# Four moves in a fused attention and MLP kernel: x emptied ahead of the masks, two stores held back, larger pieces of w_in, scores ahead of outputs

## The chip, the cores and the metric

The kernel runs on one core of a Trainium2 chip. The metric is the device time of one execution in microseconds, and less is better. Three runs of the kernel before gave a median of 215.4 us (215.04 to 215.58). One more execution, taken with the hardware profiler, took 215.47 us; every row of the trace quoted below is from that one.

## The reference

Decayed linear attention is computed over blocks, its heads are put side by side to give x of 3072 tokens by 512, and x goes through a two-layer MLP with an exact GELU. With B = 4, H = 8, S = 768, D = 64:

```python
for b in range(nb):                       # blocks of 64 positions
    intra = (qb @ kb^T * Dmask) @ vb      # lam**(i-j) below the diagonal
    inter = (qb * lam**(pos+1)) @ kv_state
    out[:, :, sl] = intra + inter
    kv_state = lam**64 * kv_state + (kb * lam**(63-pos))^T @ vb
x = out.transpose(0, 2, 1, 3).reshape(B * S, H * D)
h = x @ w_in                              # 512 x 2048
g = 0.5 * h * (1 + erf(h / sqrt(2)))
return g @ w_out                          # 2048 x 512
```

## The kernel before, in words

The sequence is cut into six groups of 128 positions. A group g holds four chunks n = 4g to 4g+3, one for each batch element. Attention of a chunk ends in a quarter (128 columns) of the transposed tile x of its group. The MLP of a group is a list of blocks, each one stretch of TensorE work: 16 blocks `mm1` (four matmuls each, then a GELU on ScalarE into `g_t`), perhaps a `rest` block for columns left out of the first `mm1` blocks, and 16 blocks `mm2` (four matmuls each; every fourth finishes 128 rows of output, which ScalarE copies to `o_sb` and SyncE's queue stores).

The order on every engine is written by hand (`manual_schedule`): each engine runs its instructions in program order. `run_blocks` walks the blocks of group g and calls, ahead of block i, whatever a dictionary lists for i. So attention of group g+1 lies between the MLP blocks of group g.

A *visit* `visit(f, d)` issues two chunks' attention matmuls in alternation: of chunk d the scores `sc` and the state products `kv`, of chunk f the outputs `o` (from its state, its masked scores `sm`, and its state in mid-chunk `mid`). VectorE then works on what the visit left in PSUM, in program order: `mask(d)` (L232), the sum `t` (L247) and its copy `mid` (L251), `empty(f)` (L284: `o` times `lam_o` into x), and the next state (L256, L258). The last visit of a group stands ahead of its last `mm2` block, and fills the last quarter of the next x.

Before a state product, GpSimd must have made `vd`, the decayed v of the chunk (L221, `decay_v`), and half of `k2`, a copy of k by half blocks (L208). From group 1 on, v of a whole group comes in four loads (`load_blocks`, L81), called V1 to V5 below; `decay_v` of any chunk of the group waits for all four.

All loads are issued by GpSimd (POOL), which also turns float32 into bf16 on the way; the list in `ask` gives their order at the start: the k, q and v of group 0, pieces of w_in (each in two halves of the partitions, L100), four pieces of w_out (L103), then k4, q4, V1, k5, q5 and so on. SyncE's queue (SP) carries the stores (L381) and, from chunk 8 on, the DMA transposes of k and q (L198, L199), in one order: two stores of group 0, the transposes of chunk 8, the other two stores of group 0, the transposes of chunk 9, and on. Each SP entry waits for its source, and all behind it wait as well.

The start (group 0) has its own forms: `scores0`, `outputs0`, `transposed` on TensorE, and matmuls on zeros (`keep_warm`, L422) that fill gaps. The first two `mm1` blocks of group 0 leave out the last 128 columns (n3 = 2), which a `rest` block adds later; `mm1` block 2 is the first that needs all four chunks of x.

Of the kernel before, what the change touches and what calls it, by code (L numbers as in the profile page):

```python
# [8 lines left out]
F32 = mybir.dt.float32  # L9
# [6 lines left out]
def kernel(  # L16
# [10 lines left out]
    nc = tc.nc  # L27
# [3 lines left out]
    C = 128  # L31
    L = 64
    NB = S // C
    HP = H // 2
# [19 lines left out]
    def bank(shape, dtype, tag, name):  # L54
        return ps.tile(shape, dtype, tag=tag, name=name, bufs=BANKS[tag])

    def half(i):
        return slice(i * 64, (i + 1) * 64)
# [9 lines left out]
    def load(n, name):  # L68
        g, b = n // B, n % B
        t = raw[n, name] = qkv_pool.tile([128, H, D], BF16, tag=name, name=f"{name}_t",  # L70
                                         bufs=B if name == "v" else 10)
        nc.gpsimd.dma_start(t, dram[name][b, :, g * C:(g + 1) * C, :].rearrange("h si d -> si h d"))  # L72

    def load_blocks(g):

        t = raw["group", g] = qkv_pool.tile([128, 2, B * HP, D], BF16, tag="vg", name="vg_t", bufs=3)
        src = v.rearrange("b (hp hi) s d -> hi s (b hp) d", hi=2)
        for u in range(2):
            for hi in range(2):
                s = g * C + u * L  # L80
                nc.gpsimd.dma_start(t[half(hi), u], src[hi, s:s + L])  # L81
# [23 lines left out]
    def ask(items):  # L105

        for item in items.split():
            name, at = item[0], item[1:]
            if name in "kqv":
                load(int(at), name)  # L110
            elif name == "V":
                load_blocks(int(at))
            else:
                (load_w_in if name == "i" else load_w_out)(*(int(x) for x in at.split("-")))

    ask("k0 q0 k1 q1 v0 k2 q2 v1 k3 q3 v2 i0-2 v3 i2-3 i3-5 i5-8 i8-12 i12-16 o0-4 o4-8 o8-12 o12-16 "
        "k4 q4 V1 k5 q5 k6 q6 k7 q7")

    idle = consts.tile([128, 512], BF16)
# [54 lines left out]
    live = {}  # L174
# [59 lines left out]
    def states(c):  # L234
        kv = c.kv = bank([128, 2, HP, D], F32, "at", "kv_ps")
        us = range(2) if c.g < NG - 1 else range(1)
        return [[(kv[half(hi), u, hp, :], c.k2[half(hi), u, hp, :], vd[c.n][half(hi), u, hp, :], True)
                 for hi in range(2)] for u in us for hp in range(HP)]
# [44 lines left out]
    def empty(c):  # L283
        nc.vector.tensor_mul(xT[c.g][:, :, c.b * C:(c.b + 1) * C], c.o, lam_o)  # L284

    def issue(*lists):

        for i in range(max(map(len, lists))):
            for pairs in lists:
                if i < len(pairs):  # L290
                    for out_, lhsT, rhs, start in pairs[i]:
                        nc.tensor.matmul(out_, lhsT, rhs, start=start, stop=True, skip_group_check=True)  # L292

    def visit(f, d, hold=False):
        f, d = (live[n] if n is not None else None for n in (f, d))
        lists = []
        if d:
            kv = states(d)
            lists.append(scores(d) + kv)
        if f:  # L300
            lists.append(outputs(f))
        issue(*lists)
        if d is None:
            empty(f)
            f = None
        if d:
            mask(d)
            next_states(d, lambda: f and empty(f), hold)


    def scores0(n):
        c = live[n]
        sc = [bank([128, HP, C], F32, "at", f"sc{hi}_ps") for hi in range(2)]
        issue([[(sc[hi][:, hp, :], c.kT[half(hi), hp, :], c.qT[half(hi), hp, :], True) for hi in range(2)]
               for hp in range(HP)])
        c.sm = work_pool.tile([128, HP, 2, C], BF16, tag="sm0", name="sm0")
        dmask_r = dmask0.rearrange("p (hp hi) i -> p hp hi i", hi=2)
        for hi in range(2):
            nc.vector.tensor_mul(c.sm[:, :, hi, :], sc[hi], dmask_r[:, :, hi, :])

    def outputs0(n):
        c = live[n]
        c.o = bank([128, HP, C], F32, "at", "o_ps")
        issue([[(c.o[half(1 - hi), hp, :], c.v[:, 2 * hp + hi, :], c.sm[:, hp, hi, :], True) for hi in range(2)]
               for hp in range(HP)])
# [4 lines left out]
        eng.tensor_mul(c.kd, c.k, lam_m[:, :, None].to_broadcast((128, H, D)))  # L330

    xT = {}

    def alloc_x(g):
        xT[g] = x_pool.tile([128, NK1, T], BF16, tag="x", name="x_t")
# [12 lines left out]
    def mlp(g, n3):  # L348

        x_t = xT[g]  # L350
        g_t = g_pool.tile([128, NK2, T], BF16, tag="g", name="g_t")

        def mm1(kf, hi=T):
            def run():
                h_ps = bank([128, T], F32, "mh", "h_ps")
                cuts = [(0, 2 * C), (2 * C, hi)] if g < 2 and kf == 0 else [(0, hi)]
                for lo, up in cuts:
                    for ki in range(NK1):
                        nc.tensor.matmul(h_ps[:, lo:up], w_in_t[:, ki, kf * 128:(kf + 1) * 128], x_t[:, ki, lo:up],  # L359
                                         start=(ki == 0 and lo == 0), stop=(ki == NK1 - 1), skip_group_check=True)  # L360
                nc.scalar.activation(g_t[:, kf, :hi], h_ps[:, :hi], ACT.Gelu)  # L361
            return run

        def rest(kfs):
            def run():
                h_ps = bank([128, len(kfs), C], F32, "mh", "h_ps")
                for i, kf in enumerate(kfs):
                    for ki in range(NK1):
                        nc.tensor.matmul(h_ps[:, i, :], w_in_t[:, ki, kf * 128:(kf + 1) * 128], x_t[:, ki, T - C:],
                                         start=(i == 0 and ki == 0), stop=(ki == NK1 - 1), skip_group_check=True)  # L370
                nc.scalar.activation(g_t[:, kfs[0]:kfs[-1] + 1, T - C:], h_ps, ACT.Gelu)
            return run

        om = {}

        def store(io, ps_, w):
            n = w.stop - w.start
            o_sb = out_pool.tile([128, n], F32, tag=f"o_{n}", name="o_sb")
            r = io * S + g * C
            nc.scalar.copy(o_sb, ps_)  # L380
            nc.sync.dma_start(out[r:r + C, w], o_sb)  # L381

        def mm2(io, part):
            def run():
                if part == 0:
                    om[io] = bank([128, d_model], F32, "mo", "o2_ps")
                for kf in range(part * 4, part * 4 + 4):
                    nc.tensor.matmul(om[io], g_t[:, kf, io * C:(io + 1) * C], w_out_t[:, kf, :],  # L388
                                     start=(kf == 0), stop=(kf == NK2 - 1))
                if part == NK2 // 4 - 1:  # L390
                    store(io, om[io], slice(0, d_model))
            return run

        def mm2_half(io, h):
            def run():
                w = slice(h * (d_model // 2), (h + 1) * (d_model // 2))
                o2 = bank([128, d_model // 2], F32, "mo", "o2_ps")
                for kf in range(NK2):
                    nc.tensor.matmul(o2, g_t[:, kf, io * C:(io + 1) * C], w_out_t[:, kf, w],  # L399
                                     start=(kf == 0), stop=(kf == NK2 - 1))  # L400
                store(io, o2, w)
            return run

        blocks = [mm1(kf, T - C if kf < n3 else T) for kf in range(NK2)]
        late = [rest(list(range(i, min(i + 4, n3)))) for i in range(0, n3, 4)]
        blocks = blocks[:n3 + 2] + late + blocks[n3 + 2:]
        if g == 0:
            blocks += [mm2(io, part) for pair in range(0, B, 2) for part in range(4) for io in (pair, pair + 1)]
        elif g == NG - 1:
            blocks += [mm2(io, part) for io in range(B - 1) for part in range(4)]  # L410
            blocks += [mm2_half(B - 1, h) for h in range(2)]
        else:
            blocks += [mm2(io, part) for io in range(B) for part in range(4)]
        return blocks
# [3 lines left out]
    def keep_warm(n, new=True):  # L418
        if new:
            idle_ps[0] = bank([128, 512], F32, "mo", "idle_ps")  # L420
        for _ in range(n):
            nc.tensor.matmul(idle_ps[0], idle[:, :128], idle, start=True, stop=True)  # L422
# [25 lines left out]
    transposed(live[3], "q", "mo", nc.scalar)  # L448
    make_lam()
    nc.scalar.activation(warm, pos, ACT.Gelu)  # L450
    outputs0(2)
    empty(live[2])
    keep_warm(1)
    scores0(3)
    keep_warm(2, new=False)


    n3 = 2
# [36 lines left out]
    visit(6, None)  # L495
    live[6].rest()
    visit(None, 7)

# [95 lines left out]
```

## Time and profile before

| what | value |
|---|---|
| median of 3 runs | 215.4 us (215.04 to 215.58) |
| profiled execution | 215.47 us |
| its span, first to last instruction | 213.7 us |
| TensorE busy (PE) | 200.6 us, 94% |
| VectorE (DVE), ScalarE (ACT), GpSimd (POOL) busy | 80.2, 90.0, 108.9 us |
| loads, queue of GpSimd | 13.64 MB, 80256 packets |
| stores and transposes, queue of SyncE | 10.50 MB, 21152 packets |
| mean granted TensorE clock | 0.989 of full speed |

Times in a view are microseconds from the first instruction. In the timeline a row has start, duration, engine, line, operation, operands and count, and in brackets how long the engine was idle before it and what ended that. In the chain of waits a row has start, length and what the time went to. A DMA issue is listed with the time from issue to landing. A table by windows has, for each stretch, its length, each engine's busy time and count of instructions, the granted TensorE clock, the DMA share, and GB/s.

### The profile page before, as it was taken

What the parts mean: (1) busy time and instruction counts of PE and PEld (TensorE: products, weight loads), DVE (VectorE), ACT (ScalarE), POOL (GpSimd) and SP (SyncE); (2) the same over time, 40 slices, a digit from 0 to 9 for tenths busy, and PEclk for the clock granted to TensorE, in tenths of its full rate; (3) what the DMA queues carried; (4) which work ended last, traced back from release to release, by engine and by line L of the source; (5) the groups of instructions that cost most, each with busy time, mean ns of one, the idle gap of its engine ahead of it and who ended that gap; (6) DMA issues with size and microseconds to landing.
All of it is one profiled execution on the core that took longest, in us unless ns stands there. A gap on an engine that the chain in (4) does not pass through costs nothing.

```text
span 213.7 us, 5227 instructions
## 1 busy us (share of the span) xinstructions
PE 200.6 (94%) x2241; PEld 99.7 (47%) x2241; DVE 80.2 (38%) x176; ACT 90.0 (42%) x161; POOL 108.9 (51%) x152
## 2 busy tenths in 40 slices
PE   7679999969999999999999799999999999999993
PEld 2345444436654444444444344444444544444452
DVE  5759102219715565725633816532330330100000
ACT  6555671429565411356311356311366221576121
POOL 8999643789759973999679969400000000000000
PEclk9969999999999999999999999999999999999998
DMA  6999999999999999999999999712100012100112
GB/s 39 145 157 162 198 206 198 155 211 94 187 109 143 139 162 127 82 148 222 165 150 133 221 180 160 80 52 98 52 2 3 0 52 98 49 3 0 49 52 95
DMA packets 101431, 24.46 MB, mean 114 GB/s; under 512 B 93600, under 2 KB 98464, under 8 KB 101408
## 3 DMA queue, kind: packets, MB, share of 16 engines
q0 software_dynamic: 80256, 13.64, 87.8%
q1 hardware_dynamic: 21152, 10.50, 24.1%
q8 instruction: 17, 0.28, 0.5%
q14 instruction: 6, 0.05, 0.1%
HBM read 27.27 MB, written 6.29 MB: 157 GB/s over the span
## 4 chain that ended last, share of the span: by engine, by line
PE 72%; DMA 11%; POOL 10%; DVE 3%; issue 1%; ACT 1%; POOLq 0%
PE h_ps L359 32%; PE o_ps L388 32%; DMA w_out_t<-in_moe_w_out_dram 7%; DMA q_t<-in_q_dram 4%; POOL w_in_t L100 3%; PE sc_ps L292 3%; PE o_ps L292 2%; POOL k_t L72 2%; POOL q_t L72 2%; POOL v_t L72 2%; PE o_ps L399 2%; PE kv_ps L292 1%; POOL w_out_t L103 1%; DVE x_t L284 1%; DVE sm L232 1%
## 5 line engine op out<-in xcount | busy, mean ns | idle before, releaser
L359 PE MATMUL h_ps<-x_t,w_in_t 128*128 128x512 bf16 (+3 forms) x392 | 84.9, 372 | 2.1 <-DVE x_t L284 1.6
L388 PE MATMUL o_ps<-w_out_t,g_t 128*128 128x512 bf16 x368 | 82.8, 379 | 0.0
L361 ACT ACTIVATE g_t<-h_ps 128x512 bf16<-128x512 f32 (+1 forms) x96 | 56.6, 591 | 35.5 <-PE h_ps L359 35.5
L359 PEld LDWEIGHTS <-w_in_t 128*128 128x128 bf16 x392 | 37.1, 98 | 44.3 <-issue 3.7
L388 PEld LDWEIGHTS <-g_t 128*128 128x128 bf16 x368 | 34.9, 98 | 40.8 <-issue 0.2
L380 ACT COPY o_sb<-o_ps 128x512 f32<-128x512 f32 (+1 forms) x25 | 14.1, 570 | 70.5 <-PE o_ps L388 68.0
L232 DVE TENSOR_TENSOR sm<-sc_ps,dmask 128x512 bf16<-128x512 f32 x20 | 13.8, 690 | 70.8 <-PE sc_ps L292 70.8
L221 POOL TENSOR_TENSOR vd<-vg_t,lam_v 128x512 bf16<-128x512 bf16 x20 | 20.9, 1047 | 15.0 <-DMA vg_t<-in_v_dram 11.8
L72 POOL DMA_DIRECT2D k_t<-in_k_dram x24 | 21.9, 910 | 2.9 <-DMA w_out_t<-in_moe_w_out_dram 2.1
L72 POOL DMA_DIRECT2D q_t<-in_q_dram x24 | 21.6, 899 | 2.3 <-DMA w_out_t<-in_moe_w_out_dram 1.9
L284 DVE TENSOR_TENSOR x_t<-o_ps,lam_o 128x512 bf16<-128x512 f32 x24 | 16.4, 682 | 9.1 <-PE o_ps L292 9.1
L81 POOL DMA_DIRECT2D vg_t<-in_v_dram x20 | 16.6, 846 | 4.3 <-DMA w_out_t<-in_moe_w_out_dram 2.8
L208 POOL COPY k<-k_t 64x256 bf16<-64x256 bf16 x38 | 15.7, 412 | 1.1
L212 DVE COPY k<-k_t 64x256 bf16<-64x256 bf16 x34 | 12.1, 356 | 0.5
L292 PEld LDWEIGHTS <-kT 64*64 64x64 bf16 (+1 forms) x352 | 7.7, 108 | 8.3 <-issue 7.9
L292 PE MATMUL sc_ps<-qT,kT 64*64 64x64 bf16 (+1 forms) x352 | 10.6, 199 | 0.5 <-ACT qT L193 0.5
L292 PE MATMUL o_ps<-sm,vg_t 64*64 64x64 bf16 x320 | 8.8, 193 | 0.1
L292 PE MATMUL kv_ps<-vd,k 64*64 64x64 bf16 x288 | 8.4, 193 | 0.3 <-ACT k L212 0.3
L258 DVE TENSOR_TENSOR state<-t,lam_c 128x256 bf16<-128x256 f32 x16 | 8.2, 511 | 0.5
L422 PE MATMUL idle_ps<-idle 128*128 128x512 bf16 x17 | 6.8, 517 | 1.2 <-DVE idle L120 1.2
L100 POOL DMA_DIRECT2D w_in_t<-in_moe_w_in_dram x12 | 7.6, 676 | 0.4 <-DMA v_t<-in_v_dram 0.2
L292 PEld LDWEIGHTS <-vg_t 64*64 64x64 bf16 x320 | 7.0, 108 | 0.2 <-issue 0.2
(62 smaller groups left out, 119.3 us busy)
## 6 DMA issues: line engine op xcount, KB each, us to landing
out_dram<-o_sb SPq DMA_DIRECT2D x23, 256.0 KB, 4.2
k_t<-in_k_dram POOLq DMA_DIRECT2D x24, 128.0 KB, 6.0
q_t<-in_q_dram POOLq DMA_DIRECT2D x24, 128.0 KB, 5.8
vg_t<-in_v_dram POOLq DMA_DIRECT2D x20, 128.0 KB, 8.0
w_out_t<-in_moe_w_out_dram POOLq DMA_DIRECT2D x4, 512.0 KB, 12.9
w_in_t<-in_moe_w_in_dram POOLq DMA_DIRECT2D x4, 256.0 KB, 7.3
v_t<-in_v_dram POOLq DMA_DIRECT2D x4, 128.0 KB, 4.8
w_in_t<-in_moe_w_in_dram POOLq DMA_DIRECT2D x4, 128.0 KB, 4.9
```

What stands on the lines that cost most here:

```text
L72: nc.gpsimd.dma_start(t, dram[name][b, :, g * C:(g + 1) * C, :].rearrange("h si d -> si h d"))
L81: nc.gpsimd.dma_start(t[half(hi), u], src[hi, s:s + L])
L100: nc.gpsimd.dma_start(w_in_t[half(1 - hi), :, f], w_in_r[hi, :, :, f])
L208: same.tensor_copy(c.k2[half(hi), hi], k_r[half(hi), :, hi, :])
L221: nc.gpsimd.tensor_mul(vd[n], of_group(n), lam_vb)
L232: nc.vector.tensor_mul(c.sm, c.sc, dmask)
L284: nc.vector.tensor_mul(xT[c.g][:, :, c.b * C:(c.b + 1) * C], c.o, lam_o)
L292: nc.tensor.matmul(out_, lhsT, rhs, start=start, stop=True, skip_group_check=True)
L359: nc.tensor.matmul(h_ps[:, lo:up], w_in_t[:, ki, kf * 128:(kf + 1) * 128], x_t[:, ki, lo:up], start=(ki == 0 and lo == 0), stop=(ki == NK1 ...
L361: nc.scalar.activation(g_t[:, kf, :hi], h_ps[:, :hi], ACT.Gelu)
L380: nc.scalar.copy(o_sb, ps_)
L388: nc.tensor.matmul(om[io], g_t[:, kf, io * C:(io + 1) * C], w_out_t[:, kf, :], start=(kf == 0), stop=(kf == NK2 - 1))
```

## The change

It has four parts.

1. **w_in.** The pieces i2-3 and i3-5 (columns 256 to 384 and 384 to 640) become one piece i2-5. Two DMA issues on GpSimd go, and two stay that are larger.
2. **x emptied first.** In a visit with both chunks, `empty(f)` comes ahead of `mask(d)`, the sum and `mid` on VectorE if f is of group 2 or later. For f of group 1 the order stays.
3. **Stores held back.** The four stores of group 0 are put on SP's queue after the last visit of group 0's MLP: behind the transposes of chunk 8, which wait for k8 and q8. Before, two of them stood ahead of these.
4. **Scores of chunk 3.** `scores0(3)` goes ahead of `outputs0(2)` on TensorE, its mask stays behind `empty(2)` on VectorE, and three matmuls on zeros that stood around it go.

```diff
-    ask("k0 q0 k1 q1 v0 k2 q2 v1 k3 q3 v2 i0-2 v3 i2-3 i3-5 i5-8 i8-12 i12-16 o0-4 o4-8 o8-12 o12-16 "
+    ask("k0 q0 k1 q1 v0 k2 q2 v1 k3 q3 v2 i0-2 v3 i2-5 i5-8 i8-12 i12-16 o0-4 o4-8 o8-12 o12-16 "
         "k4 q4 V1 k5 q5 k6 q6 k7 q7")
...
         issue(*lists)
-        if d is None:
+        if d is None or f and f.g > 1:
             empty(f)
             f = None
...
-    def scores0(n):
+    def scores0(n, mask=True):
         c = live[n]
-        sc = [bank([128, HP, C], F32, "at", f"sc{hi}_ps") for hi in range(2)]
+        c.sc = [bank([128, HP, C], F32, "at", f"sc{hi}_ps") for hi in range(2)]
...
+        if mask:
+            mask0(n)
+
+    def mask0(n):
+        c = live[n]
         c.sm = work_pool.tile([128, HP, 2, C], BF16, tag="sm0", name="sm0")
...
+    held = []
+
+    def store_held():
+        for r, w, o_sb in held:
+            nc.sync.dma_start(out[r:r + C, w], o_sb)
...
             nc.scalar.copy(o_sb, ps_)
-            nc.sync.dma_start(out[r:r + C, w], o_sb)
+            if g == 0:
+                held.append((r, w, o_sb))
+            else:
+                nc.sync.dma_start(out[r:r + C, w], o_sb)
...
     nc.scalar.activation(warm, pos, ACT.Gelu)
+    scores0(3, mask=False)
     outputs0(2)
     empty(live[2])
-    keep_warm(1)
-    scores0(3)
-    keep_warm(2, new=False)
+    mask0(3)
...
     visit(6, None)
     live[6].rest()
     visit(None, 7)
+    store_held()
```

More of the change, by code (lines that the diff above doesn't have):

```diff
@@ L308, in visit @@
             next_states(d, lambda: f and empty(f), hold)
-    def scores0(n):
+    def scores0(n, mask=True):
         c = live[n]
-        sc = [bank([128, HP, C], F32, "at", f"sc{hi}_ps") for hi in range(2)]
-        issue([[(sc[hi][:, hp, :], c.kT[half(hi), hp, :], c.qT[half(hi), hp, :], True) for hi in range(2)]
+        c.sc = [bank([128, HP, C], F32, "at", f"sc{hi}_ps") for hi in range(2)]
+        issue([[(c.sc[hi][:, hp, :], c.kT[half(hi), hp, :], c.qT[half(hi), hp, :], True) for hi in range(2)]
                for hp in range(HP)])
+        if mask:
+            mask0(n)
+    def mask0(n):
+        c = live[n]
         c.sm = work_pool.tile([128, HP, 2, C], BF16, tag="sm0", name="sm0")
@@ L318, in scores0 @@
         for hi in range(2):
-            nc.vector.tensor_mul(c.sm[:, :, hi, :], sc[hi], dmask_r[:, :, hi, :])
+            nc.vector.tensor_mul(c.sm[:, :, hi, :], c.sc[hi], dmask_r[:, :, hi, :])
     def outputs0(n):
```

## The prediction

> **What bounds the kernel now.** The page comes first: TensorE is busy for 94% of the span, so what can be won is in its gaps, 13.1 us of 213.7.
>
> ```profile
> PE 200.6 (94%) x2241; PEld 99.7 (47%) x2241; DVE 80.2 (38%) x176; ACT 90.0 (42%) x161; POOL 108.9 (51%) x152
> ```
>
> Where the gaps lie is read from TensorE's timeline: the bracket of a row is its idle time and what ended it. Three rows concern this change.
>
> ```profile
> 46.34 0.40 PE L191 MATMUL t_ps<-ident,q_t 128*128 128x128 bf16 x4 [1.84 <-DMA q_t<-in_q_dram]
> ...
> 120.52 1.67 PE L359 MATMUL h_ps<-x_t,w_in_t 128*128 128x512 bf16 x7 [1.15 <-DVE x_t L284]
> ...
> 151.85 1.45 PE L359 MATMUL h_ps<-x_t,w_in_t 128*128 128x512 bf16 x6 [0.49 <-DVE x_t L284]
> ```
>
> The last two stand where group 2 gives way to 3, and 3 to 4: the first `mm1` block needs the last quarter of x. The chain of waits, in order of time, says what VectorE does in the first of them.
>
> ```profile
> 118.16 0.69 DVE sm L232
> 118.85 0.34 DVE t L247
> ...
> 119.21 0.66 DVE mid L251
> 119.87 0.61 DVE x_t L284
> ```
>
> Mask, sum and copy of a chunk that nobody needs for 8 us run ahead of the x that TensorE waits for.
>
> The third view is GpSimd's timeline in group 1, with the chain's rows for the state products that need its work.
>
> ```profile
> 60.84 1.04 POOL L221 TENSOR_TENSOR vd<-vg_t,lam_v 128x512 bf16<-128x512 bf16 x1 [3.65 <-DMA vg_t<-in_v_dram]
> 61.83 0.85 POOL L208 COPY k<-k_t 64x256 bf16<-64x256 bf16 x2
> ...
> 67.35 0.85 POOL L208 COPY k<-k_t 64x256 bf16<-64x256 bf16 x2
> ```
>
> ```profile
> 63.38 0.25 PE kv_ps L292 x16
> ...
> 68.43 0.03 PE kv_ps L292 x2
> ```
>
> GpSimd waits 3.65 us for V2 and from there works without a gap until 68.20 (67.35 + 0.85). TensorE's kv of chunk 8 starts 0.70 after GpSimd's copy for it (62.68), and kv of chunk 9 only 0.23 after its copy (68.20). So the landing of V2 is hidden now, but by 0.2 us.
>
> **Part 2, x first.** Nothing is added or removed; two rows of order change. At 118, the outputs end at about 118.4 (last row of the visit 118.18 + 0.22). `empty` then takes 0.68 and x is ready at 119.15. TensorE's `mm2` block began at 118.33 and its four matmuls are issued at 0.216 each, so the next can start at 119.20 instead of 120.52: 1.32 won (the row says 1.15 of idle, since it counts from the modelled end of the matmul before). At 150, `mm2` began at 150.32 and is through at 151.19 against 151.85: 0.66. Sum 1.98, by the brackets alone 1.64; I take 1.9. At the turn from 1 to 2 two `mm2` blocks follow the visit and no wait is seen; from 4 to 5 there is no chunk d. What is pushed back, by `empty`'s 0.68 and about 0.25 of waiting for the outputs, is sm, t, mid and state of d; they are next read in a visit 6 or more blocks on (at 0.86 each, 5 us), and the PSUM banks that they free are asked for there too. Price: nothing, while those 5 us stand.
>
> **Part 3, the stores.** Two stores are issued at 39.94 and 40.80. k5, issued at 35.70, lands after 8.4 (44.1); q5, at 38.51, after 7.8 (46.3); k6, at 39.38, after 7.8 (47.2). Loads otherwise land 0.85 apart, so the two stores cost the loads 2.2 - 0.85 = 1.4 us, 0.7 each. Held back, q5 and all loads behind it land 1.4 earlier, and the 1.84 bracket at 46.34 shrinks by so much.
>
> But the gain has to pass GpSimd. Its chain from 43.39 (first vd of group 1, on V1's landing) to the issue of V2 at 52.10 has no gap and does not wait for these loads; it does not move. V2's four loads are issued from 52.10 to 55.38, as before, and the last lands at about 60.7. Into them now fall the held stores. On SP's queue they wait for the transposes of chunk 8: k8 lands near 49.6, q8 (issued at 47.12, and 3.9 us is the shortest landing of such a load) at 51.0; at 1.25 of issue each the queue is free at 52.3, and four stores follow at about 0.55 to 0.6. Stores 2 and 3 were there before (54.75, 55.23); 0 and 1 are new. The window from 51 to 54 is nearly empty and takes some of them:
>
> ```profile
> 43.00:47.00 4.00, 2.11 (x33) 1.08 (x33) 0.00 (x0) 0.82 (x2) 3.54 (x5) 1.00 1.94 231
> 51.00:54.00 3.00, 3.00 (x81) 1.62 (x80) 2.39 (x6) 2.86 (x7) 2.94 (x6) 1.00 0.47 94
> 57.00:61.00 4.00, 3.59 (x40) 2.00 (x34) 2.01 (x6) 2.73 (x6) 0.35 (x2) 1.00 1.90 222
> ```
>
> (The last three columns are clock, DMA share, GB/s.) A store alone lands 2.0 after its issue (those after 171 us), so store 0 is through by 54.4, before V2's bytes; store 1 mostly collides. V2's delay lies between -0.7 (store 2 slips behind it) and +1.4 (both new ones in front); I take +0.1 to +0.5 with part 1 counted, nearer the first end because of the idle window. The Trainium skill (DMA: Bandwidth & Descriptors, "Issuing engines are not separate DMA queues") says that DMAs of all queues interleave on the same 16 engines, which speaks against this part: held stores meet other loads; by that rule alone the delay is 1.4. Nobody else waits behind these stores: the next SP entry, the transpose of k9, waits for k9 at 61.5 anyway, and four of six `o_sb` buffers are held until long before the next store at 78.8.
>
> **Part 1, w_in.** GpSimd saves two issues of 0.61, 1.2 us; no load lands earlier for it, since they already queue (i5-8 lands 5.5 and 5.8 after issue, the first loads 3.9): price 0, at best -1.2. For the DMA engines: i2-3 and i3-5 landed from 17.7 to 19.8, 2.1 for 384 KB; the one pair of the new form, i5-8, took 19.8 to 22.3, 2.5. So all later loads, V1 too, slip by 0.4 (0 to 0.4), and GpSimd's chain with them; that is in V2's +0.5. `mm1` block 2 now needs the whole piece, at 17.7 + 2.5 = 20.2, where it started at 19.29 behind x: TensorE 0.9 late. The wait for q5 hides it; without that, 0.9.
>
> **Part 4, scores.** TensorE does `scores0(3)` at 15.2 (qT is copied by 15.16) in the wait for v2, and loses three matmuls of zeros. VectorE masks chunk 3 behind `empty(2)` as before, from 16.72, and the first piece of w_in still lands at 16.8 (11.72 and 5.1): nothing moves, price 0. The danger is the clock.
>
> ```profile
> 7.72:11.13 3.41, 2.06 (x35) 1.28 (x32) 2.79 (x5) 1.72 (x3) 3.41 (x5) 1.00 2.29 146
> 11.13:14.55 3.42, 3.35 (x30) 1.90 (x28) 1.82 (x4) 1.05 (x2) 3.42 (x7) 0.50 2.09 155
> 14.55:17.96 3.41, 2.34 (x28) 1.49 (x29) 2.34 (x4) 2.61 (x8) 3.09 (x6) 1.00 1.68 163
> ```
>
> After 3.41 us with 2.06 of work the clock stood at 0.50 for as long. The third stretch loses about 0.6 of its 2.34 and falls below 2.06, so the next may run at half: between 0 and 1.7 us of TensorE (3.41 / 2), about 0.6 on top of the 0.9, as it waits for w_in in much of that stretch. [...]
>
> **Sum.** TensorE comes to q5 0.9 to 1.5 late, q5 lands 1.0 earlier (1.4 - 0.4); of the bracket of 1.84 nothing or little is left, and TensorE is 0.4 to 1.0 ahead. At kv of chunks 8 and 9 GpSimd decides: V2's delay of 0.1 to 0.5 less the 0.2 of slack, 0 to +0.3. After chunk 12 GpSimd runs a chunk or more ahead, so the shift stays. Front +0.2, turns -1.9: 1.7 off the profiled execution of 215.47 (span 213.7, 1.8 around it), which is 0.07 over the median: 213.8, span 212.0.
>
> **Rivals.**
> - *The front gains too.* V2 lands up to 0.7 earlier because the stores fit in 51 to 54 or slip behind it. kv of chunk 9 can then come 0.2 to 0.9 earlier: 212.8 to 213.5. For it: DMA share 0.47 there. Against: it needs part 1 to cost nothing.
> - *The stores meet V2.* Delay 1.4 + 0.4, less 0.2: +1.6, less 1.9: 215.1. For it: the 1.4 that two stores cost at 44. Within the noise of the kernel before.
> - *Slower: the clock falls in the wait for V2.* TensorE, ahead by up to 1.0, stops at kv of chunk 8 for that and V2's delay, 1.5 to 2.8 in one place near 62; if 3.41 us hold no more than 2.06 of work, the next run at half, in dense matmuls that nothing hides: 1.7. With V2's delay of 1.4 to 1.8: 216.5 to 216.8. It decides from a stop of 1.35 on. Against: the stop of 1.84 at 44.5, in a stretch with 2.11 of 4.00, left the clock at 1.00.
> - That parts 3 or 4 do not happen is excluded by the order of the queues; that part 2 wins nothing needs another wait at 119.2, and none is seen (h_ps's banks are free).
>
> **Numbers.** Main case 58% (213.2 to 214.5), front gains 15%, stores meet V2 17%, clock 10%. A measurement of this kernel tells about 0.3%, 0.65 us: below 214.75 is faster. The first two lie there, 73%; the third is within, 17%; the last is slower, 10%. The range takes in the first three: 212.9 to 215.1.
>
> **What would show it.** Right: no bracket at the turns to groups 3 and 4; the bracket at q5 below 0.8; GpSimd's first vd of group 1's own plan (60.84) at 60.9 to 61.4, still after a wait for V2; a bracket of 0.5 to 1.5 at kv of chunk 8. Wrong: V2 landing after 62, a clock of 0.5 after 21.4, or a new bracket of over 0.3 in groups 2 to 5.

## The result and the profile after

The changed kernel took 214.52 us (median of 20 runs, 213.0 to 216.07) where the kernel before, run beside it, took 215.52 (20 runs). The ratio is 0.9944 with a 95% interval of 0.9917 to 0.997, which lies below 1: about 1.2 us less (0.0056 x 215.5), small but faster. Here and below a median is over all executions of a kernel, while a ratio and its interval leave out those that took over 1.5% longer than its fastest. The profiled execution took 213.86 us (span 212.1), against 215.47 (span 213.7) before.

The page of the kernel after begins so; its PE row lacks a few records (2211 matmuls, where 2238 weight loads are listed), so its 92% is too low:

```profile
span 212.1 us, 5187 instructions
PE 195.4 (92%) x2211; PEld 98.7 (47%) x2238; DVE 80.6 (38%) x176; ACT 89.9 (42%) x161; POOL 107.6 (51%) x150
```

**The turn from group 2 to 3.** The chain in order of time, kernel after. Where before VectorE's sm, t, mid and x stood between the visit and `mm1`, there is now only TensorE's own queue:

```profile
118.80 0.16 issue
118.96 0.81 PE o_ps L401 x3
119.77 2.40 PE h_ps L369 x11
```

VectorE's timeline, kernel after: x is first, and mask and sum come behind it.

```profile
118.90 0.69 DVE L284 TENSOR_TENSOR x_t<-o_ps,lam_o 128x512 bf16<-128x512 f32 x1 [3.71 <-PE o_ps L292]
119.50 0.68 DVE L232 TENSOR_TENSOR sm<-sc_ps,dmask 128x512 bf16<-128x512 f32 x1
120.10 0.42 DVE L247 TENSOR_TENSOR t<-kv_ps,state 128x256 f32<-128x256 f32 x1
```

From the visit before the turn to the one behind it, TensorE needs 7.68 us (118.09 to 125.77) where it needed 8.99 (117.66 to 126.65): 1.31 won. At the turn from 3 to 4 it is 7.65 (148.73 to 156.38) against 8.30: 0.65 won.

**The front.** TensorE's timeline, kernel after, with the brackets that carry it:

```profile
19.87 1.89 PE L369 MATMUL h_ps<-x_t,w_in_t 128*128 128x512 bf16 x7 [1.13 <-DMA w_in_t<-in_moe_w_in_dram]
...
44.55 0.39 PE L191 MATMUL t_ps<-ident,q_t 128*128 128x128 bf16 x4
...
62.91 0.77 PE L292 MATMUL kv_ps<-vd,k 64*64 64x64 bf16 x16 [1.33 <-POOL k L208]
...
68.85 0.22 PE L292 MATMUL sc_ps<-qT,kT 64*64 64x64 bf16 x2 [0.75 <-DMA qT<-q_t]
```

The first row is part 1's wait for the larger piece of w_in. The second is q5's transpose: the 1.84 that stood there before is gone. The third is the wait at kv of chunk 8, which the prediction had. The fourth, at the scores of chunk 9, it did not have. The chain in order of time shows where that one comes from:

```profile
55.21 9.06 DMA q_t<-in_q_dram
64.28 0.02 issue
64.29 4.52 DMA qT<-q_t
68.81 0.04 issue
68.85 0.22 PE sc_ps L292 x2
```

q9's load took 9.06 us to land (6.1 before). Then come its DMA transpose on SP's queue, 4.52 (3.56 before), and TensorE. GpSimd's timeline has the issue of V2 and its first use, in the vd of chunk 8: first the kernel before, whose vd stood at 60.84, then the kernel after.

```profile
52.10 3.31 POOL L81 DMA_DIRECT2D vg_t<-in_v_dram  x4
```

```profile
51.04 3.30 POOL L81 DMA_DIRECT2D vg_t<-in_v_dram  x4
...
61.48 1.04 POOL L221 TENSOR_TENSOR vd<-vg_t,lam_v 128x512 bf16<-128x512 bf16 x1 [5.36 <-DMA vg_t<-in_v_dram]
```

So V2 is issued 1.06 earlier and used 0.64 later: from issue to use it takes 10.44 us, where it took 8.74.

The visit of chunk 10 is 0.8 later than before in these two profiles (74.77 against 73.94), and the visit ahead of the first turn 0.4 (118.09 against 117.66). From chunk 10's visit to the end the kernel after needs 137.3 us where the kernel before needed 139.8. So in the profiles the back gains about 2.4 and the front loses 0.8: 1.6, the difference of the spans (213.7 - 212.1). One profile of each is little for the front: in three profiles with part 2 alone or a piece of it (below), whose start is that of the kernel before, this visit begins at 73.75, 74.81 and 74.82.

### The profile page after: what moved, and what is told of

Same layout as the page of the kernel before. It is cut to its first block, busy times and chain, and to the rows that moved or that the text cites. A ratio compares the mean times of both kernels' runs of the same rounds, so it can differ in the third digit from the quotient of the medians.

```text
span 212.1 us, 5187 instructions
## 1 busy us (share of the span) xinstructions
PE 195.4 (92%) x2211; PEld 98.7 (47%) x2238; DVE 80.6 (38%) x176; ACT 89.9 (42%) x161; POOL 107.6 (51%) x150
## 4 chain that ended last, share of the span: by engine, by line
PE 74%; POOL 12%; DMA 9%; issue 1%; ACT 1%; POOLq 0%
PE o_ps L401 34%; PE h_ps L369 34%; DMA q_t<-in_q_dram 4%; DMA w_in_t<-in_moe_w_in_dram 3%; POOL k_t L72 3%; PE sc_ps L292 2%; DMA qT<-q_t 2%; POOL q_t L72 2%; POOL vd L221 2%; POOL v_t L72 2%; PE o_ps L412 2%; POOL vg_t L81 2%; PE o_ps L292 1%; PE kv_ps L292 1%; POOL k L208 1%
## 5 line engine op out<-in xcount | busy, mean ns | idle before, releaser
L401 PE MATMUL o_ps<-w_out_t,g_t 128*128 128x512 bf16 x354 | 80.0, 379 | 1.7 <-issue 1.6
L212 DVE COPY k<-k_t 64x256 bf16<-64x256 bf16 x34 | 13.0, 381 | 0.5
L292 PEld LDWEIGHTS <-k 64*64 64x64 bf16 x288 | 6.5, 108 | 2.2 <-POOL k L208 1.7
L247 DVE TENSOR_TENSOR t<-kv_ps,state 128x256 f32<-128x256 f32 x16 | 6.7, 416 | 1.6 <-PE kv_ps L292 1.5
```

Of the source, the lines that this page charges most:

```text
L212: copy(c.k2[half(hi), 1 - hi], k_r[half(1 - hi), :, hi, :])
```

## The experiments

The theory after the result: part 2 earns its two us at the turns; part 1 brings the loads forward; and part 3 loses what that earns, since the held stores run beside V2, k9 and q9 and make the transposes of chunk 9 late. Then the whole without part 3 should be the best of all. The rival: group 1's loads and transposes are late as a set, whatever is moved among them, so that what is won at one wait only comes back at the next. The first four kernels take the change apart. All ran beside the kernel before (median 215.29).

### Part 2 alone

```
-        if d is None:
+        if d is None or f and f.g > 1:
             empty(f)
```

> Part 2 alone: x is emptied ahead of the masks from group 2 on, all else as before. Theory A (the turns pay): the brackets of 1.15 and 0.49 us at the turns to groups 3 and 4 go, nothing else moves; 1.6 to 2.0 us less than before, ratio 0.991 to 0.9925. Theory B (the gain of the whole change comes from the start, group 0 and 1): the turns are worth at most 0.5 us here, because another wait takes their place; ratio 0.998 or more.

Measured: 213.75, ratio 0.9905 [0.9871, 0.994], 2.0 us less. The chain at the turn has the form of the whole change:

```profile
118.86 0.16 issue
119.02 0.81 PE o_ps L388 x3
119.83 3.26 PE h_ps L359 x15
```

Part 2 alone is worth about the 1.9 that the prediction took for it (1.3 to 2.8 by the interval). By median it is better than the whole, though the two intervals overlap.

### Part 1 alone

```
-    ... v2 i0-2 v3 i2-3 i3-5 i5-8 i8-12 ...
+    ... v2 i0-2 v3 i2-5 i5-8 i8-12 ...
```

> Part 1 alone: one piece of w_in, i2-5, in place of i2-3 and i3-5. The prediction priced it at 0 for the loads, or 0.4 us late. After the whole change V1's last load landed 1.1 us earlier than before (42.1 against 43.2). Theory A (two issues of GpSimd less bring all later loads forward): V1 lands at about 42.1, q5 and V2 about 1 us earlier, and as V2 decides at the state products of chunks 8 and 9, 0.8 to 1.1 us less than before; ratio 0.995 to 0.9965. Theory B (the earlier loads come from part 3 or 4): V1 lands at 43.2 or later and the time is the same or up to 0.4 us more.

Measured: 215.86, ratio 1.0005 [0.9972, 1.0037]: no difference. In its profile the loads did come earlier. The stretch from 18 to 22 us (the last columns are clock, DMA share and GB/s) of before, then of this kernel:

```profile
18.00:22.00 4.00, 3.64 (x29) 1.92 (x28) 3.53 (x7) 2.26 (x5) 3.71 (x6) 1.00 1.20 161
```

```profile
18.00:22.00 4.00, 2.91 (x21) 1.44 (x23) 3.37 (x6) 1.09 (x2) 2.20 (x4) 1.00 1.29 203
```

GpSimd was busy for 3.71 of 4.00 us with fewer bytes moved, and for 2.20 with more, as if its issuing had been the limit. But part 3 alone (next section), which keeps the small pieces, shows 200 GB/s with GpSimd as busy as before:

```profile
18.00:22.00 4.00, 3.51 (x22) 1.60 (x22) 3.58 (x6) 1.96 (x4) 3.70 (x7) 1.00 1.31 200
```

Over all profiles, the seven with the small pieces have 161 to 200 GB/s in this stretch and use V1 first at 42.7 to 43.9 us (mean 43.2); the seven with part 1 have 197 to 204 and use it at 42.3 to 43.5 (mean 42.8). So part 1 may bring V1 0.4 forward, within the spread, and what limits this stretch stays open.

In the profile of part 1 alone V1's last load lands at 42.5 (43.2 before), q5's wait is gone, and chunk 4's visit starts at 45.22 (46.66). But two later waits on TensorE's timeline take it all back:

```profile
66.95 0.22 PE L292 MATMUL sc_ps<-qT,kT 64*64 64x64 bf16 x2 [0.34 <-DMA qT<-q_t]
...
74.51 0.22 PE L292 MATMUL sc_ps<-qT,kT 64*64 64x64 bf16 x2 [1.54 <-DMA qT<-q_t]
```

A gain of 1.4 at 45 us became a wait for the transposes of chunks 9 and 10.

### Part 3 alone

```
+            if g == 0:
+                held.append((r, w, o_sb))
+            else:
+                nc.sync.dma_start(out[r:r + C, w], o_sb)
...
     visit(None, 7)
+    store_held()
```

> Part 3 alone: the four stores of group 0 behind the transposes of chunk 8. Theory A (the stores meet V2, k9 and q9): q5 lands 1.4 us earlier, but V2's last load 0.7 to 1.5 us later than 60.7 and q9 1 to 2 us later than 62.4, so TensorE stops at the state products of chunk 8 and the scores of chunk 9; 0.5 to 1.5 us more than before, ratio 1.002 to 1.007. Theory B (holding the stores back pays): V2 at 60.7 or earlier, the time 0 to 1.4 us less.

Measured: 217.27, ratio 1.0073 [1.0039, 1.0106], 1.6 us more. TensorE arrives early at kv of chunk 8 and stops there for GpSimd, which waits for V2:

```profile
63.12 0.82 PE L292 MATMUL kv_ps<-vd,k 64*64 64x64 bf16 x16 [1.75 <-POOL k L208]
```

The windows around it show the clock falling just behind:

```profile
60.00:63.68 3.68, 1.81 (x38) 0.93 (x36) 0.69 (x1) 1.19 (x2) 1.87 (x4) 1.00 1.52 99
63.68:67.10 3.42, 3.20 (x14) 1.28 (x14) 2.19 (x6) 0.60 (x1) 3.42 (x4) 0.50 0.97 103
67.10:70.00 2.90, 2.90 (x29) 1.21 (x31) 0.00 (x0) 1.82 (x4) 2.78 (x6) 1.00 2.00 142
```

After 1.81 us of work in 3.68 the clock is 0.50 for 3.42 us, in dense matmuls. Chunk 9's visit starts at 69.87 against 67.99. This is the prediction's slower rival, with part 3 by itself.

That the held stores meet the loads shows in every profile. From V2's issue to its first use it takes 8.4 to 9.7 us in the six where the stores go out as before, and 10.3 to 11.1 in the six where they follow chunk 8's transposes: 1.5 more on average. q9 lands 5.9 to 7.5 us after its issue in the first six, and 7.9 to 9.1 in the others.

### The whole without part 3

The edit is the reverse of the one above, on the kernel after.

> The whole change without part 3: stores 0 and 1 of group 0 go out where they did before. Theory A: part 1's 1.0 us reaches the state products of chunks 8 and 9 and part 2's 1.9 us the turns; 2.6 to 3.0 us less than before (ratio 0.986 to 0.988), 1 to 1.6 us less than the whole change. Theory B (part 3 is what pays at the start): this is slower than the whole change by 0.5 us or more.

Measured: 214.13, ratio 0.9927 [0.9891, 0.9963], 1.6 us less, short of the 2.6 to 3.0 that the first theory asked for. TensorE's timeline has the stop of chunk 9's transposes here too, without any held store:

```profile
68.63 0.22 PE L292 MATMUL sc_ps<-qT,kT 64*64 64x64 bf16 x2 [1.09 <-DMA qT<-q_t]
```

So this kernel and the whole (0.9944 [0.9917, 0.997]) aren't told apart. Its windows show part 4's danger as it was described, in the place where it was put:

```profile
14.00:17.28 3.28, 1.33 (x22) 0.93 (x23) 2.10 (x4) 2.75 (x7) 3.01 (x6) 1.00 1.59 165
17.28:20.69 3.41, 3.41 (x21) 1.79 (x21) 2.39 (x5) 0.75 (x2) 2.26 (x4) 0.50 1.28 193
```

What is early at 45 us stops at chunk 9 or 10, with held stores or without. So the rival of a set of transposes that are late together gained weight, and the next runs moved the stores clear of V2 and of q9 (kernel before beside them: 215.74).

### The stores behind chunk 9's transposes, in the whole change

```
     visit(None, 7)
-    store_held()
...
-                0: [lambda: values(n), lambda: request(n + 1)],
+                0: [lambda: values(n), lambda: request(n + 1), store_held],
```

> The whole change, but the four held stores go behind the transposes of chunk 9 instead of those of chunk 8, into the stretch near 62 to 65 us where the DMA engines are nearly idle. Theory A (held stores cost what they take from V2, k9 and q9): V2's last load lands at 57 to 58 us instead of 61.3, q9 at 59 to 60 instead of 64.3; the stops of 1.33 at the state products of chunk 8 and 0.75 at the scores of chunk 9 go; 1 to 2 us less than the whole change, ratio to before 0.985 to 0.990. Theory B (the loads and transposes of group 1 are bound as a whole): V2 lands early all the same, but a stop of about the same sum comes later, at chunk 10 or 12; the time of the whole change, ratio 0.992 to 0.996.

Measured: median 218.4 over 12 runs (214.68 to 220.09). The ratio of 0.9987 [0.994, 1.0035] is over only 4 of them, so this run alone decides nothing. Its profiled execution (218.68) isn't one of the 4. In it V2's last load lands early (58.9), and TensorE stops for 4.20 us at the scores of chunk 10, as in the next run.

### The same place for the stores, with part 2 alone

```
+            if g == 0:
+                held.append((r, w, o_sb))
...
+                0: [lambda: values(n), lambda: request(n + 1), store_held],
```

> Part 2 with the stores behind the transposes of chunk 9, without parts 1 and 4. Theory A: 2.0 us for part 2 and up to 1.4 us for q5 with no store ahead of V2: 2.5 to 3.4 us less than before, ratio 0.984 to 0.988. Theory B (group 1 is bound as a whole): the time of part 2 alone, ratio 0.989 to 0.992.

Measured: 218.27, ratio 1.0111 [1.0064, 1.0159], 2.4 us more, which neither theory had. GpSimd's timeline shows V2 used 2.0 us earlier than before (60.84):

```profile
58.83 1.04 POOL L221 TENSOR_TENSOR vd<-vg_t,lam_v 128x512 bf16<-128x512 bf16 x1 [2.21 <-DMA vg_t<-in_v_dram]
```

TensorE's timeline shows what came of it, and the windows add two stretches of half clock:

```profile
76.25 0.26 PE L292 MATMUL sc_ps<-qT,kT 64*64 64x64 bf16 x2 [4.18 <-DMA qT<-q_t]
```

```profile
70.00:74.19 4.19, 2.07 (x10) 0.75 (x8) 0.97 (x2) 0.71 (x2) 4.13 (x7) 1.00 2.57 129
74.19:81.02 6.83, 4.43 (x72) 2.31 (x74) 3.11 (x8) 0.14 (x1) 2.53 (x4) 0.50 1.84 157
```

The four stores, issued from 62.10 to 63.73, meet k and q of the next chunks: k10's transpose now takes 8.92 us to land and q10's 8.03 (4.21 and 4.61 before). In both places tried, from 52 and from 62 us on, the transposes issued behind the four stores land later than before. These transposes stand on the stores' own queue, so its order may be a part of it. But the loads of k11 and q11, on GpSimd's queue, are late as well: 6.66 and 8.71 us to landing, against 4.29 and 4.51 before. The Trainium skill (DMA: Bandwidth & Descriptors, "Issuing engines are not separate DMA queues") says that transfers of all issuing engines interleave on the same 16 DMA engines; these two loads agree.

### The whole without part 4

```
-    scores0(3, mask=False)
     outputs0(2)
     empty(live[2])
-    mask0(3)
+    keep_warm(1)
+    scores0(3)
+    keep_warm(2, new=False)
```

> The whole change without part 4: the three matmuls of zeros and the old order are back. Theory A (part 4 costs a stretch of half clock in many runs, most of it hidden behind loads): the mean granted clock rises from 0.985 to 0.99 or more, the time is 0 to 0.6 us less than the whole change. Theory B (part 4 costs nothing or gains): clock and time as with the whole change, or up to 0.5 us more.

Measured: 215.32, ratio 0.996 [0.9927, 0.9992], not told apart from the whole (0.9944 [0.9917, 0.997]). Over the runs compared, the mean granted clock is 0.989 here and 0.986 and 0.984 in the two series of the whole. One half-clock stretch of 3.41 us lowers the mean of a span of 212 by 0.008 (3.41 x 0.5 / 212), so part 4 goes with a third to two thirds of such a stretch per run more (0.003 to 0.005). The profiles say the same: of the five with part 4, three have a half-clock stretch that begins between 17.2 and 18.5 us (the whole without part 3, and the two below at 17.46 and 18.49), and none of the nine without it has one there. No cost of it in time can be seen in the medians. In this kernel's profile the stop at kv of chunk 8 was 1.89 and the clock fell behind it, from 64.10 to 67.51.

### Part 2 for the fourth chunk alone

```
-        if d is None:
+        if d is None or f and f.g > 1 and f.b == B - 1:
```

> Part 2 at the last visit of a group alone (chunk f is the fourth of its group); all else as before. Theory A (the turns are all): the brackets at the turns to groups 3 and 4 are gone as with part 2 alone, and visits are as far apart as there. Theory B (each visit gains a little too): the visits of group 2 stay about 7.72 us apart as before, where part 2 alone has 7.65.

One execution: 214.1, span 212.3. The turn is the same as in part 2 alone:

```profile
118.97 0.16 issue
119.13 0.81 PE o_ps L388 x3
119.94 3.26 PE h_ps L359 x15
```

The visits of group 2 stand 7.68 apart, against 7.65 with x first everywhere: the turns make nearly all of part 2, and each other visit gains about 0.03.

The start of this kernel is that of the kernel before, but in this execution q5 landed early (44.41) and chunk 4's visit began at 44.78. TensorE's timeline then has a stop at chunk 10's transposes here too:

```profile
74.81 0.22 PE L292 MATMUL sc_ps<-qT,kT 64*64 64x64 bf16 x2 [0.57 <-DMA qT<-q_t]
```

So what is early at 45 us can stop there without parts 1, 3 and 4.

### The whole, with TensorE kept busy at kv of chunk 8

Matmuls of zeros fill the wait, so that TensorE has work in it. The last group ran beside a kernel before of 215.94.

```
-    def visit(f, d, hold=False):
+    def visit(f, d, hold=False, warm=0):
...
-            lists.append(scores(d) + kv)
+            if warm:
+                issue(scores(d))
+                keep_warm(warm)
+                lists.append(kv)
+            else:
+                lists.append(scores(d) + kv)
...
-                8: [lambda: visit(None, n)],
+                8: [lambda: visit(None, n, warm=5)],
```

> The whole change, and five matmuls of zeros (1.1 us) on TensorE between the scores and the state products of chunk 8, where it stops for V2. Theory A (in part of the executions the clock falls to half after that stop, as in the profile of part 3 alone, and this is what keeps the median 0.6 to 0.7 us over the profiled execution): no stretch of 0.5 begins between 60 and 68 us, the median is 0.3 to 0.8 us less than that of the whole change run beside it, its runs lie closer together. Theory B (the spread comes from the loads): the same median within 0.3 us, or up to 0.5 us more, as the matmuls stand in the way when V2 is early.

Measured: 215.24, ratio 0.9948 [0.9911, 0.9986], the same as the whole beside it, and its runs lie as far apart (213.68 to 216.84). No half clock begins from 60 to 68 us in its profile, so the clock in that one wait doesn't explain how far the runs of the whole lie apart. Its profile has half clock from 17.46 to 24.29, and chunk 4's visit begins at 47.32 where it began at 44.87 in the kernel after: up to there the two kernels are the same.

### Part 3 alone, kept busy there

The same edit on part 3 alone, with six matmuls.

> Part 3 alone, with six matmuls of zeros (1.3 us) between the scores and the state products of chunk 8. Theory A (of the 1.6 us that part 3 alone lost, the half clock after the stop at 63 us is the larger part): no stretch of 0.5 begins there, the time is 0.8 to 1.7 us less than with part 3 alone, ratio to before 0.999 to 1.003. Theory B (the stop itself and the later transposes make the loss): ratio 1.005 or more, as with part 3 alone.

Measured: 217.05, ratio 1.0034 [0.9993, 1.0075], between what the two theories asked for. The half clock is gone (compare part 3 alone):

```profile
60.00:63.68 3.68, 3.67 (x43) 2.00 (x41) 0.69 (x1) 1.79 (x3) 0.73 (x1) 1.00 1.75 175
63.68:67.10 3.42, 2.60 (x26) 1.39 (x27) 1.75 (x6) 0.68 (x2) 3.30 (x6) 1.00 0.48 85
```

Over the runs compared the mean clock is 0.996, against 0.990 with part 3 alone. By the two ratios the loss went from 1.6 to 0.7 us, but the intervals overlap. How much of part 3's price is clock and how much is the stop itself stays open.

### The whole again, and part 2 alone again

No edit; both ran on the chip of the two kernels above.

> The whole change once more, to stand beside the kernels of this call: ratio 0.9917 to 0.997 as measured before.

> Part 2 alone once more, beside the whole change on the same chip. Theory A (parts 1, 3 and 4 together cost something): 0.3 to 1.2 us less than the whole change. Theory B (they are worth nothing either way): within 0.3 us of it.

Measured: the whole 215.71 and 0.9952 [0.9917, 0.9986], part 2 alone 212.92 and 0.9832 [0.9798, 0.9867]. So by the medians parts 1, 3 and 4 together cost 0.8 us (0.9944 against 0.9905, intervals that overlap) to 2.6 us (0.9952 against 0.9832, intervals apart); the second figure is more than either theory had. But the two series of part 2 alone, on two chips, lie apart as well: 2.0 us less (0.9871 to 0.994) and 3.6 (0.9798 to 0.9867, over 6 runs). What of this is the chip isn't known, so a ratio here can be off by more than its interval. The whole's profile of this series has half clock from 8.25 to 15.08 and from 18.49 to 21.90.

In this profile of part 2 alone the old wait at q5 is there, and the transposes of chunks 9 and 10 are waited for by nobody (TensorE's timeline has no bracket there):

```profile
45.99 0.40 PE L191 MATMUL t_ps<-ident,q_t 128*128 128x128 bf16 x4 [1.56 <-DMA q_t<-in_q_dram]
```

The mean granted clock of this profile is 1.00. In the earlier one of part 2 alone it stood at 0.50 from 7.87 to 14.70, and that one's span was 1.0 longer. The profile of the kernel after has 1.00 throughout too: its span is 1.0 longer than this one's, and so is the way to chunk 10's visit (74.77 against 73.75), from which both need about 137.3. With the clock equal, parts 1, 3 and 4 cost 1.0 us in these two executions.

## Why the prediction was right

It was right in sign, in the mechanism of the gain and near in size: 213.8 forecast, 214.52 measured, 213.86 in the profiled execution, inside 212.9 to 215.1. That the profile came so near has luck in it: the back gained 2.4 instead of 1.9, the front lost 0.8 instead of 0.2, and the two misses cancel. By its own steps:

- **Part 2, 1.32 + 0.66.** Measured 1.31 and 0.65. The addition of durations at the turn was exact. It left out small gains at the other visits: from chunk 10's visit to the end part 2 alone takes 137.3 us against 139.8, 2.5 less where 1.9 was taken. The masks pushed back by x were waited for by nobody, as argued.
- **Part 3, q5 earlier.** q5 landed 2.5 earlier (43.78 against 46.29) and its wait vanished; 1.0 was forecast. 1.4 of it is against V1, the size forecast, and the other 1.1 is V1's own landing. But holding the stores isn't needed for it: with the stores in their old place q5 lands 1.7 behind V1 in part 1 alone and in the whole without part 3, as in the kernel after, and there the stores delay q6 instead. The held stores were issued from 52.01 to 54.97, about where the text put them.
- **Part 3, V2's delay of 0.1 to 0.5.** This term was mis-sized, and a second error hid it. V2 landed at 61.32, 0.64 later, and vd started at 61.48, just past the 60.9 to 61.4 that was named. But the text took V2's issue to stay at 52.10. It moved to 51.04 with V1's landing, and V2 took 1.70 longer from issue to use (1.5 on average over the profiles). That is the delay of the rival in which the stores meet V2, priced at 1.4. TensorE's stop of 1.33 at kv of chunk 8 lies within the 0.5 to 1.5.
- **"Nobody else waits behind these stores".** This is the sentence that failed. The text looked at the next entry on SP's queue, k9's transpose, and at when k9 had landed before. But k9 and q9 are loads on the same DMA engines, issued behind V2 at 54.31 and 55.21, while three of the four stores were issued from 53.97 on. q9 landed 1.9 later and its transpose 2.4 later. This is the new stop of 0.75, though the held stores aren't its only cause: the whole without part 3 has a stop of 1.09 in the same place. In the two profiles the front's +0.2 became +0.8, which single profiles show only roughly. The medians of the whole against part 2 alone put the price of parts 1, 3 and 4 at 0.8 to 2.6; how it divides among them isn't shown.
- **Part 1, "no load lands earlier for it".** Open. V1 came 1.1 earlier in the kernel after and 0.7 in part 1 alone, but over all profiles the gain is 0.4, within the spread. The bound of -1.2 held it. It changed the time by nothing: in its profile the next gate, the transposes of chunks 9 and 10, didn't move with it.
- **Part 1, TensorE 0.9 late at w_in.** Right: a wait of 1.13, `mm1` block 2 at 19.87 (20.2 forecast), and q5 no longer waited for.
- **Part 4, price 0, danger the clock.** The medians show no price. The fall of the clock did not occur in the profile of the kernel after, but did in three others with part 4, from 17.28, 17.46 and 18.49, where the text had put 17.96. Two of them ran past 21.4 us at half clock, which the text had named as a sign of being wrong.
- **The rivals.** That the front gains too did not happen (its price doesn't follow from its own 0.2 to 0.9, which gives 212.6 to 213.3). That the stores meet V2 happened in V2's delay, and V2's earlier issue took most of it back. The slower one did not decide the whole change: its stop was 1.33, under the 1.35 from which it was said to decide, and the 3.41 us around it held 2.08 of work. With 1.75 (part 3 alone) and 1.89 (the whole without part 4) the clock fell. But "no more than 2.06 of work" isn't the rule: the first profile of part 2 alone has a stretch with 1.80 that left the clock at 1.00 (last section).

Of "what would show it", no step had asked for the bracket of 0.75 at the scores of chunk 9; it is a new bracket over 0.3 at a chunk of group 2.

## What to carry to other kernels

When a DMA is moved, list everything that is issued behind it on any queue for as long as it runs, the loads' own consumers (here DMA transposes) included, and not only the next entry on its queue. A gain at an early wait is worth what the next two gates let through, so follow it to the next one that doesn't move. And where a stage turns over, order an engine's small operations by who waits for their results: two rows of order brought more here than all the work on loads and stores.

## What was not expected of the hardware

- **The clock changes in steps of one length, from a starting point that differs by run.** Stretches at 0.50 measure 3.41 us or twice that (6.83), and the changes of one trace lie whole steps apart: in the whole without part 4 the clock falls at 9.48 and again at 64.10, 16 steps of 3.414 later. Whether a stop trips it depends in part on how it falls into the steps. Counted on from 14.55, the kernel before has a boundary at 45.27, which divides its stop of 1.84 (44.50 to 46.34), and the clock stayed at 1.00. The 1.75 of part 3 alone (61.37 to 63.12) lies wholly in the step that ends at 63.68, and the clock fell. The work in a step doesn't decide alone: 2.06 us of it were followed by 0.50 in the kernel before (7.72 to 11.13), while 1.80 left it at 1.00 in the first profile of part 2 alone. That is its tenth step after the half clock that ends at 14.70, shown with the one behind it:

```profile
45.42:48.83 3.41, 1.80 (x40) 1.21 (x41) 1.00 (x2) 0.79 (x2) 3.27 (x6) 1.00 2.23 148
48.83:52.25 3.42, 2.93 (x116) 2.23 (x116) 3.21 (x8) 3.26 (x8) 3.22 (x6) 1.00 0.74 52
```

The Trainium skill (TensorE: Matmul & The Clock Gate, Part 1) describes the window as 3413 ns long and free-running, which these traces agree with.

- **A DMA transpose can take twice as long to land behind stores.** Those of chunk 10's k and q landed after 4.21 and 4.61 us before, and after 8.92 and 8.03 behind four stores; the shortest seen for chunks 8 to 11 before was 2.30 (k9).
